# Attention's products on unsplit fp32, P times v in two 64-column halves of the array

## The chip, the cores and the metric

The kernel runs on one core of a Trainium2 chip. Its time is the device time of one execution in microseconds. Three runs of the kernel before took 493.42, 491.84 and 490.93 us; their median is 491.84 us.

## The reference: attention, then two feed-forward blocks

Everything is fp32. Attention has 2 batches of 12 heads, 448 positions and 64 values a head:

```
scores = 0.125 * q @ k.T ; scores above the diagonal = -1e9
attn   = softmax(scores) ; x = attn @ v          -> x: 896 tokens x 768
y      = (sigmoid(x @ w_gate) * (x @ w_val)) @ w_out          (d_ff 1536)
h      = y @ w_in ; s = h * softmax(h)                        (d_ff 1024)
result = (s - mean) / sqrt(var + 1e-6) * g_ln @ w_out2        (896 x 768)
```

## The kernel before, in words

**Split products.** A product of two fp32 operands is made of three matmuls on the type fp32r: each operand is split into a high part and the remainder, and high x high, high x low and low x high are added in PSUM (`TERMS`; the product of the two remainders is left out). So every operand needs a conversion for its high part and a subtraction for its remainder.

**Attention in pairs of heads.** Two heads make a pair; there are 12 pairs. One head lies on partitions 0 to 63, the other on 64 to 127 with its keys in reversed blocks, so that the two score tiles of a pair have causal widths of 64, 192, 320 and 448 columns (`QE`). For each pair the kernel does these steps:

- `load_qk` and `load_v` bring in q, k and v on SP's queue. `prep_k_hi`, `prep_q_hi`, `prep_k_lo`, `prep_q_lo` (lines 234 to 255) split q and k into `qks` on GpSimd, the remainder of q on VectorE. `prep_v_hi` and `prep_v_lo` split v into `v2` (with a zero block of 64 columns between the two heads' columns) and `v3` on GpSimd. For pair 0, and for some steps of pair 1, other engines do it.
- `sc_mm` writes the scores in two groups (widths 448 and 64, then 320 and 192): `sc_mask` (line 354) starts each tile with bf16 matmuls that write the mask, `sc_dots` (line 367) adds three matmuls a tile and head. The two heads use different row halves of the array.
- `sc_max` (line 382; 387 for the first pairs) takes the maxima on VectorE, `sc_exp` (line 394) the exponentials and their sums on ScalarE.
- `sums`, `recips`, `rs_rows`, `rs_bcast` turn the sums into reciprocals and lay them out along the columns by way of a buffer in memory.
- `tr_mm` (line 437) transposes P in four units of four 128x128 blocks; `tr_hi` (line 444) copies a unit's high part to SBUF on ScalarE, `tr_lo` (helper `sub`, line 231) subtracts the remainder on VectorE.
- `pv_mm` (line 468) multiplies by v in eight chunks of in all 21 matmuls over the whole 128 columns of the array: three of 448 columns, and for each of three key blocks and each head three of 384, 256 or 128 columns. For one head's block, the other head's 64 columns of weights are zeros.
- `x_mul` (line 474) multiplies by the reciprocals; `x_hi` (line 223) and `x_lo` split the result into `xy`.

**Order of work.** The order is written out by hand: `STEPS` gives for each engine the step at which a function of pair p is issued, with eight steps a pair (`PER`), and a loop goes through all steps. The first two or three pairs' start is written out ahead of the loop. On TensorE, a period of eight steps holds the scores of pair p, the transposes of pair p - 1 between P times v of pair p - 2. PSUM's eight banks are shared as two for transposes (`ps_t`), two for x (`ps_x`) and two pairs for scores (`ps_s`).

**Weights beside attention.** The feed-forward weights arrive as raw 32-bit words in chunks (768 KB each). `bits_steps` puts the words together on ScalarE and VectorE and asks for the next chunk; `chunk_hi` and `chunk_lo` split it. The first two chunks are asked for at steps 44 and 52; the work on the first four starts at step 88. `early_tiles` (line 500) puts 36 products of the first gate and value tile, those of batch 0, between the last pairs' products, at most two a step. When they are through, the gate and value products proper (line 641) follow.

**After attention** come the gate and value products (line 641), `w_out` (line 671), `w_in` (line 703), the softmax and normalization, and the last product (line 764). All of this is TensorE's without gaps.

Of the kernel before, what the change touches and what calls it, by code (L numbers as in the profile page):

```python
# [23 lines left out]
NQ = 4  # L24
# [19 lines left out]
def attn_moe_moe2(ctx: ExitStack, tc: tile.TileContext, qk, v, w_gv, w_out, w_in2, w_out2, g_ln, out):  # L44
# [48 lines left out]
    pos = {"dma": 0, "bits": 0}  # L93
# [100 lines left out]
    with ExitStack() as actx:  # L194
        qkr = actx.enter_context(tc.tile_pool(name="qkr", bufs=2, side="right"))
        qks = actx.enter_context(tc.tile_pool(name="qks", bufs=2, side="right"))
# [4 lines left out]
        ps_t = actx.enter_context(tc.tile_pool(name="ps_t", bufs=2, space=PSUM, reuse_waits="tile"))  # L201
        ps_x = actx.enter_context(tc.tile_pool(name="ps_x", bufs=2, space=PSUM, reuse_waits="tile"))
# [3 lines left out]
        qk_raw, qk_sp = {}, {}  # L206


        def load_qk(p):
            if p < NH // 2:  # L210
                r = qkr.tile([128, 2, S], F32, tag="qkr", name="qkr")
                both = qk[2 * p:2 * p + 2].rearrange("a d i s -> (a d) i s")
                for i in (1, 0) if p == 0 else (slice(0, 2),):
                    nc.sync.dma_start(out=r[:, i], in_=both[:, i])
                qk_raw[p] = r

        def load_v(p):
            if p < NH // 2:
                nc.sync.dma_start(out=v_raw[p % 2], in_=v[p])

        def on(eng, out, in_):
            if eng == 'A':
                nc.scalar.copy(out=out, in_=in_)
            elif eng == 'P':
                nc.gpsimd.tensor_scalar(out=out, in0=in_, scalar1=1.0, scalar2=1.0, op0=ALU.mult, op1=ALU.mult)
            else:
                nc.vector.tensor_copy(out=out, in_=in_)


        def sub(eng, out, a, b):  # L230
            (nc.gpsimd if eng == 'P' else nc.vector).tensor_tensor(out=out, in0=a, in1=b, op=ALU.subtract)  # L231


        def prep_q_hi(p, eng='P'):
            if eng == 'P':
                nc.gpsimd.tensor_scalar(out=qk_sp[p][:, 1], in0=qk_raw[p][:, 0], scalar1=0.125, scalar2=1.0,
                                        op0=ALU.mult, op1=ALU.mult)
            else:
                nc.scalar.activation(out=qk_sp[p][:, 1], in_=qk_raw[p][:, 0], func=AF.Copy, scale=0.125)

        def prep_k_hi(p, eng='P'):
            qk_sp[p] = qks.tile([128, 4, S], FR, tag="qks", name="qks")
            on(eng, qk_sp[p][:, 0], qk_raw[p][:, 1])

        def prep_k_lo(p):
            sub('P' if p else 'D', qk_sp[p][:, 3], qk_raw[p][:, 1], f32(qk_sp[p][:, 0]))
            if 0 < p < 3:
                load_qk(p + 2)

        def prep_q_lo(p):  # L250
            t = qk_sp[p]
            nc.vector.scalar_tensor_tensor(out=t[:, 2], in0=qk_raw[p][:, 0], scalar=0.125, in1=f32(t[:, 1]),
                                           op0=ALU.mult, op1=ALU.subtract)
            if p > 2:
                load_qk(p + 2)

        def v_parts(p):
            return (v_raw[p % 2][:, 0:3].rearrange("p j (a d) -> p j a d", a=2),
                    *(v2[p % 2][:, i].rearrange("p j (a d) -> p j a d", a=3)[:, :, 0:3:2] for i in range(2)))

        def prep_v_hi(p):
            r, hi, lo = v_parts(p)
            on('P', hi, r)
            on('P', v3[p % 2][:, 0], v_raw[p % 2][:, 3])

        def prep_v_lo(p):
            r, hi, lo = v_parts(p)
            sub('P', lo, r, f32(hi))
            sub('P', v3[p % 2][:, 1], v_raw[p % 2][:, 3], f32(v3[p % 2][:, 0]))
            load_v(p + 2)  # L270
# [3 lines left out]
        v_raw = [one.tile([128, NQ, 2 * D], F32, name=f"vr{i}") for i in range(2)]  # L274
        nc.vector.memset(idle, 0.0)
        warm = one.tile([1, 8], F32, name="warm")
        nc.vector.memset(warm, 0.0)
        nc.scalar.activation(out=warm, in_=warm, func=AF.Exp)
# [19 lines left out]
        zero = one.tile([128, 3 * D], F32, name="zero")  # L298
        nc.vector.memset(zero, 0.0)

        v2 = [one.tile([128, 2, 3, 3 * D], FR, name=f"v2_{i}") for i in range(2)]

        v3 = [one.tile([128, 2, 2 * D], FR, name=f"v3_{i}") for i in range(2)]
# [9 lines left out]
        def zeros(i):  # L313
            for a in range(2):
                nc.scalar.copy(out=v2[i][:, a, :, D:2 * D], in_=zero.rearrange("p (j d) -> p j d", j=3))

# [7 lines left out]
        zeros(0)  # L324
        prep_k_hi(0, 'D')
        prep_q_hi(0, 'A')
        prep_k_lo(0)
        prep_q_lo(0)
# [3 lines left out]
        zeros(1)  # L332
# [4 lines left out]
        def sc_mask(p, g):  # L337
            if p < 2 and g == 0:
                both = [ps_x.tile([128, 512], F32, tag="x", name="s") if p else
                        ps_t.tile([128, 512], F32, tag="t", name="s") for _ in range(2)]  # L340
# [17 lines left out]
        def sc_dots(p, g):  # L358
            t = qk_sp[p]
            flat = t.rearrange("p c s -> p (c s)")  # L360
# [73 lines left out]
        def tr_mm(p, u):  # L434
            ps = ps_tr[p, u] = ps_t.tile([128, 512], F32, tag="t", name="t")
            for c, k in tr_blocks(u):
# [3 lines left out]
        def tr_hi(p, u):  # L440
            if p not in pt_t:
                pt_t[p] = ptp.tile([128, 2, 4, 512], FR, tag="pt", name="pt")
            w = tr_width(u)
            nc.scalar.copy(out=pt_t[p][:, 0, u, :w], in_=ps_tr[p, u][:, :w])  # L444

        def tr_lo(p, u):
            w = tr_width(u)
            sub('D', pt_t[p][:, 1, u, :w], ps_tr.pop((p, u))[:, :w], f32(pt_t[p][:, 0, u, :w]))
# [3 lines left out]
        CHUNKS = ('00 00', '00 11', '11 11', '13 13 13', '21 21', '21 12', '12 12 23', '23 23 22 22 22')  # L452
        pv_terms = {}

        def pv_mm(pr, chunk):
            if chunk == 0:
                ps_pv[pr] = ps_x.tile([128, 512], F32, tag="x", name="x")[:, :S]
                pv_terms.update({w: iter(TERMS) for w in ('00', '11', '12', '13', '21', '22', '23')})
            ps = ps_pv[pr]
            words = CHUNKS[chunk].split()  # L460
            for n, w in enumerate(words):
                sec, j = int(w[0]) - 1, int(w[1])
                a, c = next(pv_terms[w])
                q0 = 128 * j - D if j else 0
                u, c0 = {0: (0, 0), 1: (1 + sec, 0), 2: (3, 256 * sec), 3: (1 + sec, 384)}[j]

                l = v2[pr % 2][:, a, j - 1, (1 - sec) * D:(3 - sec) * D] if j else v3[pr % 2][:, a]
                nc.tensor.matmul(out=ps[:, q0:], lhsT=l, rhs=pt_t[pr][:, c, u, c0:c0 + S - q0],  # L468
                                 start=(chunk == 0 and n == 0), stop=(chunk == 7 and n == len(words) - 1),
                                 skip_group_check=True)  # L470
# [5 lines left out]
        def x_hi(pr):  # L476
            b, m = divmod(pr, NP)
            on('A', xy[m][:, 0, b * S:(b + 1) * S], xf_t[pr])

        def x_lo(pr):  # L480
            b, m = divmod(pr, NP)
            sl = slice(b * S, (b + 1) * S)
            sub('P', xy[m][:, 1, sl], xf_t.pop(pr), f32(xy[m][:, 0, sl]))
# [4 lines left out]
        def early_tiles():  # L488
# [20 lines left out]
        PER = 8  # L509
        early = early_tiles()  # L510
# [5 lines left out]
            *((13 + n, 'E', lambda p, n=n: pv_mm(p, n)) for n in range(len(CHUNKS))),  # L516
            (16, 'A', lambda p: tr_hi(p, 3)), (24, 'A', x_hi, 0, NPR - 1), (22, 'A', x_hi, NPR - 1),
            (1, 'A', lambda p: sc_exp(p, (3,), (0,)), 2),
            (9, 'A', lambda p: tr_hi(p, 0), 1),
            (1, 'A', lambda p: sc_exp(p, (3,), (1,)), 2), (2, 'A', lambda p: sc_exp(p, (0,)), 2),  # L520
            (12, 'A', lambda p: tr_hi(p, 1), 1), (5, 'A', lambda p: sc_exp(p, (2,)), 1),
            (14, 'A', lambda p: tr_hi(p, 2)), (6, 'A', lambda p: sc_exp(p, (1,)), 1),
            (-1, 'D', lambda p: sc_max(p, 3, 0), 2, 3),
            (0, 'D', lambda p: sc_max(p, 3, 0), 3), (16, 'D', lambda p: tr_lo(p, 3)),
# [310 lines left out]
```

## Time and profile before

| | us |
|---|---|
| median of three runs | 491.84 |
| the profiled execution, device time | 492.44 |
| its span | 490.7 |
| busy: TensorE matmul / weight load | 481.4 / 439.8 |
| busy: VectorE / ScalarE / GpSimd | 327.5 / 221.2 / 119.9 |
| moved by DMA | 55.6 MB, 113 GB/s in the mean |

The profile is one execution. The span runs from its first instruction to its last; 1.74 us of the device time lie outside it. Matmuls overlap in the array, so a matmul's own duration is longer than the time until the next one starts, and the busy share of TensorE counts as busy also where it could be denser. The pace of its instructions is read from the chain of waits, which lists for each stretch how long a run of instructions took until the next run began.

### The profile page before, as it was taken

How to read it: one execution, taken by the hardware profiler on the slowest of the kernel's cores; microseconds unless marked ns; L12 is line 12 of the kernel's file. 1: busy time of each engine (PE TensorE's matmuls, PEld its weight loads, DVE VectorE, ACT ScalarE, POOL GpSimd, SP SyncE). 2: the span in 40 equal slices, each digit the busy share in tenths (PEclk: the TensorE clock that was granted, in tenths of full speed). 3: DMA queues.
4: the chain of work that ended last, by engine and by line, in shares of the span. 5: the costliest groups of instructions: out<-in, count | busy, mean ns of one | idle time of the engine just before them, and what ended most of it. 6: DMA issues, size and time to landing. Idle time of an engine off the chain costs nothing.

```text
span 490.7 us, 7583 instructions
## 1 busy us (share of the span) xinstructions
PE 481.4 (98%) x2907; PEld 439.8 (90%) x2907; DVE 327.5 (67%) x508; ACT 221.2 (45%) x471; POOL 119.9 (24%) x190
## 2 busy tenths in 40 slices
PE   8999989899999999999999999999999999999997
PEld 7899878799999999999999999999988888899996
DVE  7888879985757777977777756767725988811110
ACT  6988868753343453453354232343321424333111
POOL 5869597410000000000000000000051778510000
PEclk9999999999999999999999999999999999999999
DMA  6344642233232354453345234453331121001001
GB/s 192 104 158 140 226 132 86 84 126 112 105 128 92 123 172 142 159 170 113 108 168 161 97 107 164 137 160 128 122 127 63 66 86 45 0 33 64 33 32 66
DMA packets 15685, 55.60 MB, mean 113 GB/s; under 512 B 2720, under 2 KB 4768, under 8 KB 15648
## 3 DMA queue, kind: packets, MB, share of 16 engines
q1 hardware_dynamic: 15648, 55.11, 33.9%
q8 instruction: 23, 0.38, 0.3%
q14 instruction: 14, 0.11, 0.1%
HBM read 52.30 MB, written 2.80 MB: 112 GB/s over the span
## 4 chain that ended last, share of the span: by engine, by line
PE 90%; DVE 4%; ACT 3%; DMA 2%; issue 0%; SPq 0%; POOL 0%; ACTq 0%
PE gv L641 34%; PE pm L671 18%; PE po L764 12%; PE h L703 12%; PE x L468 5%; PE t L437 3%; PE s L367 3%; DVE sum L382 2%; PE gv L500 2%; ACT p L394 2%; PE tp L746 1%; DVE pt L231 1%; DMA qkr<-in_qk_dram 1%; PE s L354 0%; DMA rb<-rd 0%
## 5 line engine op out<-in xcount | busy, mean ns | idle before, releaser
L641 PE MATMUL gv<-xy,hl 128*128 128x448 f32 x828 | 168.1, 365 | 0.0
L641 PEld LDWEIGHTS gv<-xy,hl 128*128 128x128 f32 x828 | 155.5, 188 | 12.2
L671 PE MATMUL pm<-g,hl 128*128 128x448 f32 x432 | 87.7, 365 | 0.0
L671 PEld LDWEIGHTS pm<-g,hl 128*128 128x128 f32 x432 | 81.2, 188 | 6.4
L688 POOL TENSOR_SCALAR t<-t,g_sb 128x768 f32<-128x768 f32 x8 | 9.0, 1125 | 247.7 <-PE pm L671 247.7
L134 DVE TENSOR_TENSOR hl<-t,hl 128x768 fp32r<-128x768 f32 x36 | 34.8, 968 | 40.8 <-ACT hl L131 39.0
L764 PE MATMUL po<-wo,lt 128*128 128x384 f32 x336 | 60.7, 340 | 0.0
L703 PE MATMUL h<-wi,xy 128*128 128x512 f32 x252 | 59.3, 396 | 0.0
L764 PEld LDWEIGHTS po<-wo,lt 128*128 128x128 f32 x336 | 58.7, 188 | 0.2 <-POOL wo L693 0.2
L703 PEld LDWEIGHTS h<-wi,xy 128*128 128x128 f32 x252 | 47.1, 188 | 11.4
L117 DVE SCALAR_TENSOR_TENSOR t<-raw,t 128x768 int32<-128x768 int32 (+1 forms) x56 | 52.6, 939 | 1.8
L120 DVE SCALAR_TENSOR_TENSOR t<-raw,t 128x768 int32<-128x768 int32 (+1 forms) x56 | 52.0, 929 | 1.7
L112 ACT ACTIVATE raw<-raw 128x768 f32<-128x768 f32 (+1 forms) x56 | 48.0, 865 | 9.8 <-DMA raw<-in_wo_dram 5.8
L468 PE MATMUL x<-pt,v 128*128 128x384 f32 (+3 forms) x252 | 51.0, 324 | 0.0
L394 ACT ACTIVATE p<-s,sum 128x320 f32<-128x320 f32 (+3 forms) x92 | 43.5, 491 | 11.9 <-DVE sum L382 11.0
L468 PEld LDWEIGHTS x<-pt,v 128*128 128x128 f32 x252 | 37.0, 190 | 1.6
L231 DVE TENSOR_TENSOR pt<-t,pt 128x512 fp32r<-128x512 f32 (+1 forms) x48 | 31.9, 665 | 3.1 <-ACT pt L444 3.0
L171 DVE TENSOR_TENSOR lt<-tp,lt 128x512 fp32r<-128x512 f32 x14 | 9.7, 689 | 36.4 <-ACT lt L170 36.4
L131 ACT CAST hl<-t 128x768 fp32r<-128x768 f32 x36 | 30.0, 833 | 4.8 <-PE pm L671 4.2
L115 DVE TENSOR_SCALAR t<-raw 128x768 int32<-128x768 int32 (+1 forms) x56 | 30.2, 539 | 2.6 <-ACT raw L112 2.6
L183 ACT ACTIVATE wk<-gv 128x448 f32<-128x448 f32 x23 | 11.3, 542 | 44.3 <-PE gv L641 44.3
L382 DVE TENSOR_REDUCE sum<-s 128x2 f32<-128x640 f32 (+3 forms) x44 | 28.3, 683 | 4.0 <-PE s L367 3.9
(97 smaller groups left out, 493.6 us busy)
## 6 DMA issues: line engine op xcount, KB each, us to landing
raw<-in_gv_dram SPq DMA_DIRECT2D x24, 768.0 KB
raw<-in_wo_dram SPq DMA_DIRECT2D x20, 768.0 KB
raw<-in_wi_dram SPq DMA_DIRECT2D x12, 512.0 KB
qkr<-in_qk_dram SPq DMA_DIRECT2D x11, 448.0 KB
vr<-in_v_dram SPq DMA_DIRECT2D x12, 256.0 KB
rb<-rd SPq DMA_DIRECT2D x24, 112.0 KB
out_dram<-o SPq DMA_DIRECT2D x6, 384.0 KB
rd<-rs32q SPq DMA_DIRECT2D x48, 1.0 KB
```

Of the source, the lines that this page charges most:

```text
L112: nc.scalar.activation(out=w1.bitcast(F32), in_=w1.bitcast(F32), func=AF.Copy, scale=2.0 ** -112)
L117: nc.vector.scalar_tensor_tensor(out=tt, in0=w1, scalar=-2 ** 31, in1=tt, op0=ALU.bitwise_and, op1=ALU.bitwise_or)
L120: nc.vector.scalar_tensor_tensor(out=tt, in0=w0, scalar=29, in1=tt, op0=ALU.logical_shift_right, op1=ALU.bitwise_or)
L134: nc.vector.tensor_tensor(out=lo, in0=t_t.pop(it), in1=f32(hi), op=ALU.subtract)
L231: (nc.gpsimd if eng == 'P' else nc.vector).tensor_tensor(out=out, in0=a, in1=b, op=ALU.subtract)
L382: nc.vector.reduce_max(out=sum_t[p % 3][:, 8 + 2 * i:10 + 2 * i], in_=ps_both[p, i], axis=AX.X, negate=True)
L394: nc.scalar.activation(out=p_t[p % 2][:, POFF[i] + (1 - e) * n:POFF[i] + (2 - e) * n], in_=ps_sc[p, i][1 - e], func=AF.Exp, bias=mx, scale ...
L468: nc.tensor.matmul(out=ps[:, q0:], lhsT=l, rhs=pt_t[pr][:, c, u, c0:c0 + S - q0], start=(chunk == 0 and n == 0), stop=(chunk == 7 and n == ...
L641: nc.tensor.matmul(out=ps[i, b], lhsT=w[:, a, cs], rhs=xy[kk][:, x, b * S:(b + 1) * S], start=(kk == 0 and a == 0 and x == 0), stop=(kk == ...
L671: nc.tensor.matmul(out=ps[b], lhsT=w[:, a, cs], rhs=g_t[kk][:, x, b * S:(b + 1) * S], start=(kk == 0 and a == 0 and x == 0), stop=(kk == N ...
L703: nc.tensor.matmul(out=h[:, n * 512:(n + 1) * 512], lhsT=xy[kk][:, a, tk], rhs=wi[n * NK + kk][:, c], start=(kk == 0 and i == 0), stop=(kk ...
L764: nc.tensor.matmul(out=ps[n], lhsT=lts[k // 4][:, a, k % 4], rhs=wo[k][:, c, cs], start=(k == 0 and i == 0), stop=(k == NF2 - 1 and i == 2))
```

## The change

- q and k go into the scores unsplit, as fp32: one matmul for three in `sc_dots`. k is read where it landed; q is scaled by 0.125 into `q_sc`, with 64 columns of zeros ahead of it, which the 128-column weights of the narrowest tile reach into. The conversions and subtractions for q and k are gone.
- v goes into P times v unsplit, from where it landed, and transposed P is copied unsplit: `tr_copy` takes the place of `tr_hi` and `tr_lo`; units 0 and 1 are copied by VectorE, 2 and 3 by ScalarE.
- `pv_mm` has seven matmuls: one of 448 columns over the whole array, and for each of three key blocks one matmul a head with 64 columns of weights, each writing its own half of the partitions.
- Three banks for transposes and one for x, in place of two and two. The first scores of pair 1 take one bank of each.
- Buffers: three of q and k as they land, and three of v, in place of two each.
- Steps move: P times v is issued in two chunks (steps 17 and 18), copies, reciprocals, sums, loads of q, k and v have new steps, and the work on the first weight chunks starts at step 86 in place of 88.
- The first two raw weight chunks are loaded in seven parts at steps 34 to 82, in place of whole at 44 and 52.
- For pair 0, q is loaded ahead of k; VectorE scales it. The 26 small matmuls ahead of the first transposes write into those transposes' own bank.

The diff, cut to its core:

```diff
-    pos = {"dma": 0, "bits": 0}
+    pos = {"dma": 2, "bits": 0}
+    def dma_part(c, lo, hi):
+        if c not in raw_t:
+            raw_t[c] = ring.tile([128, 2 * CH], I32, tag="raw", name="raw")
+        cs = slice(lo * CH // 2, hi * CH // 2)
+        nc.sync.dma_start(out=raw_t[c][:, cs], in_=src[c][0].bitcast(I32)[:, cs])
...
-        ps_t = actx.enter_context(tc.tile_pool(name="ps_t", bufs=2, space=PSUM, reuse_waits="tile"))
-        ps_x = actx.enter_context(tc.tile_pool(name="ps_x", bufs=2, space=PSUM, reuse_waits="tile"))
+        ps_t = actx.enter_context(tc.tile_pool(name="ps_t", bufs=3, space=PSUM, reuse_waits="tile"))
+        ps_x = actx.enter_context(tc.tile_pool(name="ps_x", bufs=1, space=PSUM, reuse_waits="tile"))
...
-                for i in (1, 0) if p == 0 else (slice(0, 2),):
+                for i in (0, 1) if p == 0 else (slice(0, 2),):
...
+        def prep_q(p, eng=nc.gpsimd):
+            eng.tensor_scalar(out=q_sc[p % 2][:, D:], in0=qk_raw[p][:, 0], scalar1=0.125, scalar2=1.0,
+                              op0=ALU.mult, op1=ALU.mult)
...
-                for m, (cq, ck) in enumerate(((1, 0), (1, 3), (2, 0))):
-
-                    for e in range(2):
-                        rows = slice(e * D, (e + 1) * D)
-                        nc.tensor.matmul(out=ps_sc[p, i][1 - e], lhsT=flat[rows, cq * S + n - 128:cq * S + n],
-                                         rhs=t[rows, ck, S - n:] if e else t[rows, ck, :n], start=False, stop=(m == 2), skip_group_check=True)
+                for e in range(2):
+                    rows = slice(e * D, (e + 1) * D)
+                    nc.tensor.matmul(out=ps_sc[p, i][1 - e], lhsT=q_sc[p % 2][rows, n - D:n + D],
+                                     rhs=k[rows, S - n:] if e else k[rows, :n], start=False, stop=True, skip_group_check=True)
...
-        def pv_mm(pr, chunk):
-            if chunk == 0:
+        def pv_mm(pr, *blocks):
+            if 0 in blocks:
                 ps_pv[pr] = ps_x.tile([128, 512], F32, tag="x", name="x")[:, :S]
...
+            for j in blocks:
                 q0 = 128 * j - D if j else 0
...
+                for e in range(2) if j else (0,):
+                    d = slice(e * D, (e + 1) * D) if j else slice(0, 2 * D)
+                    u, c0 = {0: (0, 0), 1: (2 - e, 0), 2: (3, 256 * (1 - e)), 3: (2 - e, 384)}[j]
+                    nc.tensor.matmul(out=ps_pv[pr][d, q0:], lhsT=v_raw[pr % 3][:, (j - 1) % NQ, d],
+                                     rhs=pt_t[pr][:, u, c0:c0 + S - q0],
+                                     start=(j == 0), stop=(j == 2), skip_group_check=True)
...
+        FIRST_RAW = {34: (0, 0, 1), 42: (0, 1, 2), 50: (0, 2, 3), 58: (0, 3, 4),
+                     66: (1, 0, 1), 74: (1, 1, 3), 82: (1, 3, 4)}
...
+            (17, 'E', lambda p: pv_mm(p, 0, 1)), (18, 'E', lambda p: pv_mm(p, 3, 2)),
+            (16, 'A', lambda p: tr_copy(p, 3, 'A')),
+            (1, 'A', lambda p: sc_exp(p, (3,)), 2), (2, 'A', lambda p: sc_exp(p, (0,)), 2),
+            (5, 'A', lambda p: sc_exp(p, (2,)), 1), (6, 'A', lambda p: sc_exp(p, (1,)), 1),
+            (23, 'A', x_hi), (15, 'A', lambda p: tr_copy(p, 2, 'A')),
+            (8, 'D', recips), (-1, 'D', lambda p: sc_max(p, 3, 0), 2, 3), (0, 'D', lambda p: sc_max(p, 3, 0), 3),
             (2, 'D', lambda p: sc_max(p, 2), 2), (3, 'D', lambda p: sc_max(p, 1), 2),
+            (12, 'D', lambda p: tr_copy(p, 0, 'D'), 1), (21, 'D', x_mul), (14, 'D', lambda p: tr_copy(p, 1, 'D'), 1),
+            (7, 'P', sums, 1), (-8, 'P', prep_q, 3), (24, 'P', x_lo),
+            (8, 'S', rs_rows), (8, 'S', rs_bcast), (-2, 'S', lambda p: load_qk(p + 2), 1), (11, 'S', lambda p: load_v(p + 2)),
...
-            if s in (44, 52):
-                dma_next()
+            if s in FIRST_RAW:
+                dma_part(*FIRST_RAW[s])
...
-                e = s - 88 - 8 * c
+                e = s - 86 - 8 * c
```

## Rows read from the trace of the kernel before

**Rows 1.** The page: busy time by engine; granted clock in 40 slices.

```profile
PE 481.4 (98%) x2907; PEld 439.8 (90%) x2907; DVE 327.5 (67%) x508; ACT 221.2 (45%) x471; POOL 119.9 (24%) x190
...
PEclk9999999999999999999999999999999999999999
```

**Rows 2.** Windows: stretch, length, busy us (instructions) by engine, clock, DMA share, GB/s.

```profile
30.32:37.59 7.27, 7.27 (x79) 6.52 (x81) 6.36 (x13) 6.21 (x22) 6.53 (x11) 1.00 0.40 134
...
23.09:83.43 60.34, 58.42 (x601) 52.17 (x602) 51.32 (x97) 48.73 (x165) 46.55 (x71) 1.00 0.46 147
83.43:107.31 23.88, 21.99 (x167) 20.17 (x166) 20.87 (x33) 16.50 (x41) 9.53 (x12) 1.00 0.29 97
107.31:490.70 383.39, 379.92 (x1909) 348.98 (x1907) 237.08 (x336) 137.77 (x204) 47.41 (x73) 1.00 0.32 106
```

**Rows 3.** Waits of TensorE, 23.09 to 83.43 us: total us, times, longest.

```profile
PE t L437 <- DVE pt L231: 1.9, 3, 1.2
```

**Rows 4.** Chain of waits, one period: start us, us until the next, what.

```profile
30.32 0.19 PE s L354 x6
30.51 0.94 PE s L367 x12
31.45 0.13 PE s L354 x8
31.59 0.84 PE s L367 x12
32.42 0.48 PE x L468 x3
32.91 0.46 PE t L437 x4
33.36 0.65 PE x L468 x4
34.01 0.44 PE t L437 x4
34.45 0.94 PE x L468 x8
35.38 0.44 PE t L437 x4
35.82 0.79 PE x L468 x4
36.61 0.63 PE t L437 x4
37.23 0.35 PE x L468 x2
```

**Rows 5.** Chain of waits in the drain: three 128-column products, sixteen gate products.

```profile
99.99 0.28 PE x L468 x3
...
104.08 3.23 PE gv L500 x16
```

**Rows 6.** Groups by shape, 30.32 to 37.59 us: count, busy us, mean ns.

```profile
L444 ACT CAST pt<-t 128x512 fp32r<-128x512 f32 x3 | 1.8, 600 | 0.0
...
L231 DVE TENSOR_TENSOR pt<-t,pt 128x512 fp32r<-128x512 f32 x3 | 2.1, 684 | 0.0
L252 DVE SCALAR_TENSOR_TENSOR qks<-qkr,qks 128x448 fp32r<-128x448 f32 x2 | 1.3, 665 | 0.0
```

**Rows 7.** Chain of waits in the start.

```profile
1.63 4.46 DMA qkr<-in_qk_dram
...
6.11 0.59 ACT qks L239
...
7.35 0.68 DVE mx L387 x2
...
8.12 0.61 ACT p L394
```

**Rows 8.** Timeline of the start: pair 0's q; in brackets the idle time and its releaser.

```profile
3.97 0.58 ACT L239 ACTIVATE qks<-qkr 128x448 fp32r<-128x448 f32 x1 [0.23 <-DMA qkr<-in_qk_dram]
```

More of the change, by code (lines that the diff above doesn't have):

```diff
@@ L218, in load_v @@
             if p < NH // 2:
[L219 to L231, printed above, removed]
@@ L234, in prep_q_hi @@
[L234 to L243, printed above, removed]
@@ L245, in prep_k_lo @@
[L245 to L270, printed above, removed]
+                nc.sync.dma_start(out=v_raw[p % 3], in_=v[p])
+        def prep_q(p, eng=nc.gpsimd):
+            eng.tensor_scalar(out=q_sc[p % 2][:, D:], in0=qk_raw[p][:, 0], scalar1=0.125, scalar2=1.0,
+                              op0=ALU.mult, op1=ALU.mult)
@@ L272, in attn_moe_moe2 @@
         for p in range(2):
             load_qk(p)
-        v_raw = [one.tile([128, NQ, 2 * D], F32, name=f"vr{i}") for i in range(2)]
+        q_sc = [one.tile([128, D + S], F32, name=f"qs{i}") for i in range(2)]
+        v_raw = [one.tile([128, NQ, 2 * D], F32, name=f"vr{i}") for i in range(3)]
         nc.vector.memset(idle, 0.0)
@@ L277, in attn_moe_moe2 @@
         nc.vector.memset(warm, 0.0)
+        for i in range(2):
+            nc.vector.memset(q_sc[i][:, :D], 0.0)
         nc.scalar.activation(out=warm, in_=warm, func=AF.Exp)
@@ L297, in attn_moe_moe2 @@
                                            in1=mask0[rows, rows], op0=ALU.mult, op1=ALU.add)
[L298 to L303, printed above, removed]
         sum_t = [one.tile([128, 16], F32, name=f"sum{i}") for i in range(3)]
@@ L323, in attn_moe_moe2 @@
         keep_warm(ps[:, 0], 31)
[L324 to L328, printed above, removed]
+        prep_q(0, nc.vector)
         load_qk(2)
@@ L338, in sc_mask @@
             if p < 2 and g == 0:
-                both = [ps_x.tile([128, 512], F32, tag="x", name="s") if p else
-                        ps_t.tile([128, 512], F32, tag="t", name="s") for _ in range(2)]
+                both = [ps_x.tile([128, 512], F32, tag="x", name="s") if p and e else
+                        ps_t.tile([128, 512], F32, tag="t", name="s") for e in range(2)]
             else:
@@ L438, in tr_mm, with tr_copy @@
                                     ident if c >= 0 else identx)
-        def tr_hi(p, u):
+        def tr_copy(p, u, eng):
             if p not in pt_t:
-                pt_t[p] = ptp.tile([128, 2, 4, 512], FR, tag="pt", name="pt")
+                pt_t[p] = ptp.tile([128, 4, 512], F32, tag="pt", name="pt")
             w = tr_width(u)
[L444 to L448, printed above, removed]
+            dst, src_ = pt_t[p][:, u, :w], ps_tr.pop((p, u))[:, :w]
+            if eng == 'A':
+                nc.scalar.copy(out=dst, in_=src_)
+            else:
+                nc.vector.tensor_copy(out=dst, in_=src_)
@@ L477, in x_hi @@
             b, m = divmod(pr, NP)
-            on('A', xy[m][:, 0, b * S:(b + 1) * S], xf_t[pr])
+            nc.scalar.copy(out=xy[m][:, 0, b * S:(b + 1) * S], in_=xf_t[pr])
         def x_lo(pr):
@@ L482, in x_lo @@
             sl = slice(b * S, (b + 1) * S)
-            sub('P', xy[m][:, 1, sl], xf_t.pop(pr), f32(xy[m][:, 0, sl]))
+            nc.gpsimd.tensor_tensor(out=xy[m][:, 1, sl], in0=xf_t.pop(pr), in1=f32(xy[m][:, 0, sl]), op=ALU.subtract)
             x_done.add(pr)
```

59 lines of the change are left out of this document (9 added, 50 removed).

## The prediction

> **What bounds the kernel now.** I read the page first: TensorE (PE) is busy in 98% of the span and its granted clock is full in all 40 slices [rows 1]. So time is lost or won by what TensorE is given to do and by the few moments when it waits. The windows by stage [rows 2] show where the change can act. The last 383.39 us (from 107.31 us on) are the two feed-forward blocks, whose code stays; TensorE's list of waits has no entry there. Attention has three stages: a start until the scores of pair 3 begin (23.09 us), eight periods until those of pair 11 begin (60.34 us), and a drain with the first gate products between (23.88 us). The list of waits says how little TensorE waits in the eight periods: 1.9 us in three waits, all of transposes for the subtraction that frees their bank [rows 3]. A period without a wait is in the chain of waits [rows 4], 7.27 us from mask to mask, every piece TensorE's. By kind: masks 0.19 + 0.13 = 0.32 us; scores 0.94 + 0.84 = 1.78 (24 matmuls); transposes 0.46 + 0.44 + 0.44 + 0.63 = 1.97, of which 0.2 in the last group is waiting; P times v 0.48 + 0.65 + 0.94 + 0.79 + 0.35 = 3.21 (21 matmuls). In the same window VectorE is busy 6.36 us, ScalarE 6.21, GpSimd 6.53 [rows 2]: all three would be next if TensorE alone got faster.
>
> **Part by part: TensorE.** The price of a column comes from the four 448-column products of 0.79 us [rows 4]: 0.79 / 1792 = 0.44 ns. A whole-array instruction of 128 columns takes 0.44 / 4 = 0.11 us [rows 4], about twice its 128 columns, so below 250 columns something else, as I read it the weight load, sets the pace. The two heads' score products lie side by side: 448 + 64 columns in three terms are 1536 columns, 0.68 us if the heads overlap and 1.35 if not, and 0.94 was measured.
>
> *How many streams an unsplit product takes* no row shows. Lower end: one, as the four-byte transposes pass at the same 0.11 us as split products of 128 columns. Upper end: four, one for each product of two halves; the kernel's three terms are these without the smallest. I take four, the nearest to the row of three terms, which is the only one of nearly full precision.
>
> The Trainium skill prices the same thing: "FP8 and Floating Point Precision", TensorE Precision Notes, gives a true FP32 product four passes through the array. No run here shows it; by it the period below stays as it is.
>
> Scores: 448 + 64 + 320 + 192 = 1024 columns a head, 4 x 1024 x 0.44 = 1.80 us if the heads lie side by side as now. To it comes what streams don't explain: now 0.94 - 0.68 = 0.26 and 0.84 - 0.68 = 0.16 us a group. With eight matmuls for 24, I take 0.15 a group (ends 0 and 0.26): 2.10 us, 0.32 more than now.
>
> P times v: one whole product of 448 columns and three pairs of halves of 384, 128 and 256: 1216 columns, 4 x 1216 x 0.44 = 2.14 us if halves lie side by side. Were they one after the other, 768 columns more: 3.49. No row shows two column halves; the nearest, the two row halves of the scores, overlap. I take the overlap and, for the run's end where one half still streams alone, 0.22 us: 2.36.
>
> Changing the shape of the array: three 128-column products just behind the scores take 0.48 us [rows 4], three elsewhere 0.28 [rows 5], so going from halves to the whole costs 0.20; the way back shows nothing (0.35 us for two products of 384 columns, with 0.34 to expect). Each pair gains one such change each way: 0.22 us taken, ends 0 and 0.4.
>
> The Trainium skill warns of this: "TensorEngine Tiling (Array Packing)", Tiling Modes, Key Properties, says that changing the mode, not only the tile, drains the engine. The trace agrees, with 0.48 against 0.28 us.
>
> Masks stay (0.32). Transposes stay at 16, 1.76 us without the 0.2 of waiting: a third bank lies between a transpose and the copy that frees it. New period: 0.32 + 2.10 + 1.76 + 2.36 + 0.22 = 6.76 us, 0.51 less than 7.27.
>
> **The other engines.** ScalarE loses two of the four copies of transposed P (0.60 us the wider one [rows 6], the other a little less): 6.2 - 1.1 = 5.1 us a period. VectorE loses four subtractions (2.6, three of them 2.1) and the q remainder (the window holds two, 1.3), and gains the two copies, priced by the subtraction's 0.68 us [rows 6], the nearest row (ends 0.4 and 0.8): 6.4 - 3.9 + 1.3 = 3.8 us. GpSimd loses all splitting of k and v and keeps the scaling of q, the sums and one subtraction, 2 us. All lie under 6.76, so I cost these at nothing; were TensorE below about 5.1 us, ScalarE would bound. One bank for x in place of two: the next pair's whole product waits for this pair's multiplication by the reciprocals. That follows some 2 us behind the halves and has most of a period in hand; behind a late one would stand all of TensorE's queue. On SP's queue the reads of v are now issued where P times v has ended, behind the broadcast of reciprocals; raw weights go in seven parts of 192 to 384 KB for two of 768, and each is issued 8 steps after the last. The third buffers cover both (a pair's q and k are asked for two pairs ahead), so I count nothing, at worst one late landing (some 2 us).
>
> **Start.** The first maximum is taken at 7.35 us: VectorE's queue has pair 1's q remainder ahead of it, which waits for ScalarE's 0.59 us and a transfer that lands at 6.1; the first exponential follows at 8.12 [rows 7]. In the changed kernel nothing of pair 1 stands ahead on either engine. Pair 0's second half is there at 3.97 us [rows 8]; q comes first now, and its scaling (some 0.6) ends about when k lands. Two heads of 512 columns in four streams take 0.9 us and some skew, so the first maximum is at 5.3 and the first exponential at 6.0: 2.1 us earlier. From there ScalarE leads; two copies fewer on it give another 1.1. P times v of pair 0 saves little against longer scores of three pairs. I take -3.0 us (ends -1 and -4.5).
>
> **Drain.** Three P times v save 3 x (3.21 - 2.36 - 0.22) = 1.9, one set of scores adds 0.3. The gate products stay: 0.20 us each (sixteen in 3.23 us [rows 5]), 36 in all. The conversion of the first four weight chunks starts two steps earlier on a VectorE without P's subtractions, but it is also squeezed by a shorter stage (20.87 of 23.88 us busy now [rows 2]); I leave the stage's other waits where they are: -1.6 us (ends -4 and +1).
>
> **Sum.** Start -3.0. Periods: 8 x 6.76 = 54.1, and 1 us of waits kept of 60.34 - 58.16 = 2.2 now: 55.1 - 60.34 = -5.2. Drain -1.6. Together -9.8 us, from the profiled execution's 492.44 (span 490.7 and 1.74 around it): 482.6. The median of the runs is 0.6 lower than the profiled one, so I predict 482.
>
> **Rivals.**
> *Halves of P times v go one after the other* (slower side). The period grows by 1.35 less the 0.2 of skew to 7.9: periods 63.7 (+3.4), start -1.9, drain +1.9, together +3.4: 495 us against the median. It decides once the halves cost 0.5 us more than side by side, for that is all that a period saves. For it: no row shows two column halves at once, and each half needs its own stream of P. Against it: row halves overlap in the scores.
> *An unsplit product takes two streams.* Scores 1.1 us, P times v 1.25, period 4.7 on TensorE; ScalarE's 5.1 and its waits then make 5.4: 8 x 5.4 is 17 less, start -4, drain -4.5: 466. For it: four-byte transposes at 0.11 us. Against it: a transpose needs no arithmetic.
> *TensorE's saving turns into waits*, for copies, late reciprocals through memory, or the first weight chunks: the period falls only to 7.0 with 1 us of waits kept (57 us, -3.3), start -1, drain 0: 488. For it: ScalarE and VectorE have waited for each other in most of these stages, and the drain's VectorE is 87% busy. Against it: both lose work in every period.
> *The scores' heads cease to overlap*, or the longer weight loads of unsplit products stand open: 1.8 us more a pair, period 8.6, 8 x 1.3 less the waits = +9, start and drain +2: 503. For it: below 250 columns the load already sets the pace. Against it: streams grow longer, which covers more load.
>
> **How the numbers follow.** Chances: forecast 0.45, halves in turn 0.17, two streams 0.10, waits 0.18, open loads or heads in turn 0.10. The forecast's own range is 476 to 488. With the unknown streams and halves the range is 469 to 496, which leaves out the 503 and most of the 466. A measurement of this kernel tells 0.5% (2.5 us) from no change. Faster: 0.43 of the forecast, 0.10 of two streams, 0.14 of the waits: 0.67. Same: 0.02 + 0.03 + 0.04 of the halves: 0.09. Slower: 0.13 of the halves, 0.10, 0.01: 0.24.
>
> **What would show it.** In the changed profile's chain: scores of a period near 2.1 us (1.1: two streams; 3.9: heads in turn), P times v near 2.4 (3.5: halves in turn), mask to mask 6.8 us; the halves' two records of one block starting within one stream of each other; the first exponential near 6.0 us; pair 3's scores near 20; the first product of line-641 kind (gate tiles) near 97.5 us, and from there on 383 us as before. The prediction is wrong if an unsplit product is not four streams, if halves don't overlap, or if TensorE's list of waits grows beyond some 4 us in attention.

## The result, and the profile after

The changed kernel took 487.31 us in the median of 12 runs (486.16 to 490.83), the kernel before 492.55 in runs beside it: a ratio of 0.9897 (95% interval 0.9877 to 0.9917). It is 5.2 us faster, about half of the 10 that were forecast. The profiled execution took 489.1 us, 1.8 more than the median, so its stages show somewhat less of the gain.

The windows by stage (stretch, length, busy us and instructions by engine in the order PE, PEld, DVE, ACT, POOL, then clock, DMA share, GB/s); the second and third begin at the masks of pair 3 and of pair 11, and the third ends where the last of the drain's own gate products does, at two closing matmuls of line 181 ahead of the gate tiles' regular loop:

```profile
28.19:34.69 6.50, 6.50 (x64) 4.18 (x66) 4.93 (x10) 5.35 (x21) 1.91 (x3) 1.00 0.45 160
21.68:75.75 54.07, 52.34 (x485) 33.67 (x486) 35.31 (x71) 41.68 (x152) 15.35 (x24) 1.00 0.45 147
75.75:104.06 28.31, 24.12 (x144) 15.60 (x143) 20.53 (x30) 15.27 (x39) 5.42 (x7) 0.88 0.39 132
...
104.06:487.30 383.24, 379.92 (x1908) 348.88 (x1907) 236.16 (x334) 137.65 (x204) 47.41 (x73) 1.00 0.32 106
```

Against [rows 2]: the start is 1.41 us shorter (21.68 for 23.09), the eight periods 6.27 (54.07 for 60.34), the rest equal to 0.15 us; but the drain is 4.43 us longer (28.31 for 23.88), at a mean granted clock of 0.88. Together that is -3.4 us, what the profiled executions differ by (489.1 and 492.44), and the drain is where the rest of the forecast gain went. A period of its own takes 6.50 us, less than the 6.76 that I had worked out.

TensorE's waits in the periods, then in the drain (total, times, longest):

```profile
PE t L381 <- DVE pt L392: 1.7, 3, 1.2
...
PE gv L436 <- ACT hl L137: 2.7, 1, 2.7
PE t L381 <- DVE pt L392: 1.5, 2, 0.7
```

The three waits of the periods stand at 56.6 us (0.16), 64.5 (1.23) and 71.4 (0.33); earlier there is none. So something grows late from period to period. VectorE's waits from 21 to 84 us, so in the periods and the first 8 us of the drain, say what:

```profile
DVE xf L410 <- DMA rb<-rd: 17.1, 7, 3.4
```

It waits for reciprocals, which travel by way of memory: rows of sums are written (L350), then read back by a broadcast (L356), both from SP's queue. SP's timeline (start us, us, engine, line, instruction; L99 a raw weight part, L223 v, L218 q and k), and the chain of waits at the end of the second round:

```profile
66.67 1.09 SPq L356 DMA_DIRECT2D rb<-rd  x2
67.80 0.59 SPq L99 DMA_DIRECT2D raw<-in_gv_dram  x1
68.49 0.38 SPq L223 DMA_DIRECT2D vr<-in_v_dram  x1
68.91 0.42 SPq L218 DMA_DIRECT2D qkr<-in_qk_dram  x1
69.38 1.34 SPq L350 DMA_DIRECT2D rd<-rs32q  x4
73.99 1.09 SPq L356 DMA_DIRECT2D rb<-rd  x2
```

```profile
70.42 3.49 DMA rd<-rs32q
```

The reader is to see a ring: broadcast, three loads (192 + 256 + 448 KB, 0.9 MB), four row writes, and then a hole of 3.3 us, in which SP stands until the rows have landed (3.49 us after the last one's issue began). Only then can the next broadcast go. From broadcast to broadcast that is 73.99 - 66.67 = 7.3 us; the four rounds before it, from the broadcasts at 36.79, 44.02, 51.66, 59.49 and 66.67 us, took 7.2 to 7.8, the two before those, without a raw part, 6.4 and 6.6. TensorE's period is 6.50. So each round with a raw part adds to the lag of the reciprocals, six of the seven waits above and 14.2 of their 17.1 us lying in the eight periods. VectorE waits for them in its queue ahead of P's copies and of the weight words, and from 56 us on TensorE waits too. Over the run SP waits this long for rows (total, times, longest):

```profile
SPq L356 <- DMA rd<-rs32q: 33.2, 15, 3.4
```

The chain in the drain:

```profile
77.27 3.04 DMA rd<-rs32q
...
80.88 3.38 DMA rb<-rd
...
84.38 0.62 DVE xf L410
85.01 0.87 DVE t L126
...
85.90 0.84 ACT hl L137
...
86.79 1.11 PE gv L436 x2
...
88.76 2.97 PE x L404 x6
```

The first weight chunk's last step on VectorE (L126) stands behind a multiplication that waits for reciprocals. TensorE idles for 2.7 us up to 86.79, and then runs at 1.2 GHz: the granted clock is 0.50 from 88 to 92 us, and the first part of P times v takes 2.97 us where its like at 97.68 takes 1.55.

### The profile page after: what moved, and what is told of

It reads as the page before. It is cut to its first block, busy times and chain, and to the rows that moved or that the text cites. A ratio compares the mean times of both kernels' runs of the same rounds, so it can differ in the third digit from the quotient of the medians.

```text
span 487.3 us, 7096 instructions
## 1 busy us (share of the span) xinstructions
PE 476.5 (98%) x2727; PEld 412.7 (85%) x2727; DVE 305.1 (63%) x472; ACT 207.6 (43%) x441; POOL 72.0 (15%) x121
## 4 chain that ended last, share of the span: by engine, by line
PE 87%; DMA 5%; SPq 3%; DVE 2%; ACT 1%; issue 1%; POOL 0%; DVEq 0%; ACTq 0%; POOLq 0%
PE gv L564 34%; PE pm L594 18%; PE po L687 12%; PE h L626 12%; DMA rd<-rs32q 3%; PE x L404 2%; PE gv L436 2%; PE s L309 2%; PE t L381 2%; DMA rb<-rd 1%; PE tp L669 1%; ACT p L336 1%; SPq L350 1%; DVE sum L324 1%; SPq L356 1%
## 5 line engine op out<-in xcount | busy, mean ns | idle before, releaser
L126 DVE SCALAR_TENSOR_TENSOR t<-raw,t 128x768 int32<-128x768 int32 (+1 forms) x56 | 51.2, 913 | 1.6
L336 ACT ACTIVATE p<-s,sum 128x320 f32<-128x320 f32 (+3 forms) x92 | 42.2, 484 | 10.1 <-DVE sum L324 8.1
L121 DVE TENSOR_SCALAR t<-raw 128x768 int32<-128x768 int32 (+1 forms) x56 | 31.2, 557 | 2.8 <-ACT raw L118 2.8
L404 PE MATMUL x<-pt,vr 128*64 128x384 f32 (+3 forms) x168 | 30.5, 425 | 0.0
L309 PE MATMUL s<-qkr,qs 64*128 64x448 f32 (+3 forms) x192 | 28.0, 416 | 0.0
L381 PE MATMUL t<-ident,p 128*128 128x128 f32 x180 | 25.3, 279 | 1.3 <-DVE pt L392 0.9
```

The costliest lines, as they stand in the source:

```text
L126: nc.vector.scalar_tensor_tensor(out=tt, in0=w0, scalar=29, in1=tt, op0=ALU.logical_shift_right, op1=ALU.bitwise_or)
L309: nc.tensor.matmul(out=ps_sc[p, i][1 - e], lhsT=q_sc[p % 2][rows, n - D:n + D], rhs=k[rows, S - n:] if e else k[rows, :n], start=False, st ...
L336: nc.scalar.activation(out=p_t[p % 2][:, POFF[i] + (1 - e) * n:POFF[i] + (2 - e) * n], in_=ps_sc[p, i][1 - e], func=AF.Exp, bias=mx, scale ...
L381: nc.tensor.transpose(ps[:, max(c, 0):max(c, 0) + 128], p_t[p % 2][:, k:k + 128], ident if c >= 0 else identx)
L404: nc.tensor.matmul(out=ps_pv[pr][d, q0:], lhsT=v_raw[pr % 3][:, (j - 1) % NQ, d], rhs=pt_t[pr][:, u, c0:c0 + S - q0], start=(j == 0), stop ...
```

## The experiments

Theory A: SP's round binds. Rivals: B, the weight conversion that starts two steps earlier fills VectorE; C, the loads' bytes delay the small transfers wherever they are issued.

**Loads between rows and broadcast.** `raw_part` issues the weight part that falls to a pair, one a pair from pair 3 on; it, v, q and k go behind the rows' writes, so that these land while SP issues loads. (v goes out five steps later for that, q and k two.)

```diff
-            (8, 'S', rs_rows), (8, 'S', rs_bcast), (-2, 'S', lambda p: load_qk(p + 2), 1), (11, 'S', lambda p: load_v(p + 2)),
+            (8, 'S', rs_rows), (8, 'S', raw_part), (16, 'S', lambda p: load_v(p + 2)), (0, 'S', lambda p: load_qk(p + 2), 1),
+            (8, 'S', rs_bcast),
```

> Edit to the changed kernel: on SP's queue the loads of a period (raw weight part, v, q and k) are issued between the rows of reciprocals and their broadcast, instead of behind the broadcast and so just ahead of the next rows. Theory A (SP's round is the bound: four row writes, 3.2 us until they land behind some 0.9 MB of loads, broadcast, loads; 7.2 to 7.8 us with a raw part against TensorE's 6.50; the late reciprocals hold VectorE, then TensorE, then let its clock fall): rows land within 2 us of the last issue, all eight periods take 6.5 us (52 to 53 in all, for 54.07), the 2.73 us wait for the first weight chunk and the stretch at half clock go, the drain falls from 28.3 to 24 to 25.5 us; 481 to 483 us against 487.3. Theory B (VectorE's weight conversion, started two steps earlier, is what the drain waits for): periods as in A, drain still 27 to 28, 485 to 486. Theory C (the loads' bytes delay the small transfers wherever they are issued): no change, 487.

Measured 480.74 us (0.9747, 0.9709 to 0.9785). Its windows and TensorE's waits:

```profile
21.07:73.11 52.04, 52.04 (x486) 33.51 (x487) 37.94 (x73) 42.26 (x157) 15.34 (x24) 1.00 0.60 184
73.11:95.80 22.69, 21.28 (x143) 14.36 (x143) 19.42 (x28) 14.02 (x33) 5.72 (x7) 1.00 0.38 111
```

```profile
PE gv L436 <- ACT hl L137: 1.4, 1, 1.4
```

And SP's wait for rows, over the run, to set beside the 33.2 us of the changed kernel:

```profile
SPq L356 <- DMA rd<-rs32q: 4.1, 7, 1.6
```

Eight periods of 6.50 us without a wait, the drain 22.7 us at full clock, less than the 24 to 25.5 expected. One of its rounds on SP:

```profile
41.40 1.31 SPq L350 DMA_DIRECT2D rd<-rs32q  x4
42.76 0.36 SPq L99 DMA_DIRECT2D raw<-in_gv_dram  x1
...
44.64 1.09 SPq L356 DMA_DIRECT2D rb<-rd  x2
```

The broadcast goes 1.9 us after the last row is issued (1.5 to 2.2 in the seven rounds with a raw part), and the hole is 0.6 us here. The same instructions on every engine, in another order on one queue, are worth 6.6 us by the medians. B can't explain that, as the conversion starts at the same step. Of C the form falls in which any load costs its time: the same bytes are moved. The changed kernel was not run again beside this one, but two edits below that leave the loads behind the broadcast measured 487.02 and 486.77 us in the same series.

**Raw parts out of the periods.** Both chunks go whole, at the loop's first two steps.

```diff
-        FIRST_RAW = {34: (0, 0, 1), 42: (0, 1, 2), 50: (0, 2, 3), 58: (0, 3, 4),
-                     66: (1, 0, 1), 74: (1, 1, 3), 82: (1, 3, 4)}
+        FIRST_RAW = {0: (0, 0, 4), 1: (1, 0, 4)}
```

> Edit to the changed kernel: the first two raw weight chunks are loaded whole at the first two steps of the loop (about 9 us), so that no raw part is in the eight periods; SP's order is otherwise as in the changed kernel. Theory A: SP's round goes back to the 6.4 to 6.6 us that it took in the changed kernel before the raw parts began, no drift, no wait above 0.3 us for copies; start up to 1 us longer; drain 24 to 25.5; 481 to 484 us. Theory B: drain still 27 to 28, 485 to 486. Theory C agrees with A here (fewer bytes in the periods), so this run speaks on B alone.

481.96 us (0.9769, 0.9730 to 0.9808), as A expects. Without the raw part the rounds from 42 to 69 us take 6.3 to 6.9 us, TensorE waits in none of the periods, and they are 6.50 us again. C agrees with A here, so this run speaks against B alone.

**Raw chunks whole, as before**, at their steps of before.

```diff
+        FIRST_RAW = {44: (0, 0, 4), 52: (1, 0, 4)}
```

> Edit to the changed kernel: the first two raw chunks are loaded whole at steps 44 and 52, as in the kernel before, instead of in seven parts. Theory A: two of SP's rounds take 8.5 to 10 us instead of seven that take 7.2 to 7.8, the lag is about the same (some 5 us) and the other rounds at 6.4 to 6.6 hardly recover it: 486 to 488 us, with the waits for copies starting earlier, about two periods behind step 44. If parts were the whole cause (number of issues, not bytes and order): 483 to 484. Theory B: 487.

487.02 us (0.9881, 0.9834 to 0.9928). Parts or whole makes no difference that these runs can tell. Two rounds of 8.6 and 8.9 us (broadcasts at 42.21, 50.83 and 59.73) build up the same lag as five of 7.2 to 7.8: in both kernels some 4.5 us more than as many periods (17.5 for 13.0, and 37.2 for 32.5). TensorE's waits did not start earlier, as had been expected: the first, of 1.5 us, ends at 64.5 us. This run also shows what the bytes do. From the end of the last row's issue to the broadcast it is 2.8 and 3.0 us in the changed kernel's two rounds with v, q and k alone ahead of the rows, 3.1 to 3.6 in the five after them with 192 KB of raw weights more, 4.5 and 3.9 here with 768 KB, and at most 1.5 to 2.2 with the loads behind the rows. So the rows land later the more was issued just ahead of them. The rest of a longer round is the issue of the raw part itself, 0.69 us (67.80 to 68.49 above).

**Conversion from step 88**, as before.

```diff
+            e = s - 88 - 8 * c
```

> Edit to the changed kernel: the conversion of the first weight chunks starts at step 88, as in the kernel before, instead of 86. Theory A: VectorE is held by late reciprocals either way, so the first gate product waits at least as long: 487 to 489 us. Theory B (the conversion started too early stands ahead of attention's copies): the drain falls by 2 us or more, 484 to 485.

486.77 us (0.9868, 0.9821 to 0.9915), not to be told from the changed kernel. B had forecast 484 to 485. TensorE waits there for a copy on ScalarE (2.5 us) in place of the weight chunk.

**Only the raw parts ahead of the broadcast**; v, q and k stay behind it.

```diff
-            (8, 'S', rs_rows), (8, 'S', rs_bcast), ...
+            (8, 'S', rs_rows), (8, 'S', raw_part), (8, 'S', rs_bcast), ...
```

> Edit to the changed kernel (487.3 us): only the raw weight parts move ahead of the broadcast of reciprocals; v, q and k stay behind it, just ahead of the next rows. Theory A1 (the rows land late because they queue behind bytes issued just ahead of them): the rows have 0.7 MB ahead of them instead of 0.9 to 1.1, and SP's round goes to the 6.4 to 6.7 us of the rounds without a raw part: 481 to 483.5 us. Theory A2 (any load behind the broadcast is too much): rounds of 7 us remain, 485 to 487.

482.07 us (0.9765, 0.9733 to 0.9797): rounds of 6.4 to 7.1 us (broadcasts at 36.53, 42.91, 49.31, 56.39 and 63.09 us), a little longer than the period in the middle; the slack between the engines takes that up, as it does in the kernel with the raw parts early.

**The rows from GpSimd's queue.**

```diff
-                nc.sync.dma_start(out=rows[:, b:b + 32], in_=rs_q[p % 2][b:b + 8])
+                nc.gpsimd.dma_start(out=rows[:, b:b + 32], in_=rs_q[p % 2][b:b + 8])
```

> Edit to the changed kernel: the four row writes are issued from GpSimd's queue instead of SP's; loads and broadcast stay on SP in the same order. Theory A1 with queueing in one queue: rows no longer stand behind SP's loads, land 1.5 to 2.5 us after their issue, SP's round falls by 2 us or more and no longer binds: 481 to 483 us. If it is the shared engines' bytes and not the queue: rows land as late as before (3.2 us), only SP's 1.3 us of issuing goes, round 6.0 to 6.5, 482 to 485. If issuing from GpSimd is dear (some 1 us each): its queue then holds q's scaling and the sums, 485 to 490.

482.03 us (0.9760, 0.9733 to 0.9786). From its timeline (start us, us, engine, line, instruction):

```profile
42.05 2.14 POOL L350 DMA_DIRECT2D rd<-rs32q  x4 [0.78 <-DVE rs32q L345]
...
47.42 1.09 SPq L356 DMA_DIRECT2D rb<-rd  x2
```

The last row is issued at 44.19 and the broadcast goes at 47.42, 3.2 us later. Over the seven rounds with a raw part this is 2.6 to 4.4 us, and it is 3.5 and 3.8 in the two rounds ahead of them, which have none. So rows land late from another queue too, but this run doesn't tell whether the bytes under way hold them, as C has it, or a slower write from GpSimd's queue. What it does show is that the rows no longer wait for their turn behind SP's broadcast and loads: GpSimd issues each set as soon as VectorE has the reciprocals (the bracket), 6.4 to 6.5 us apart. The seven rounds from broadcast to broadcast (35.65 to 81.09 us) take 4.7 to 7.8 us, 6.5 in the mean, TensorE's period.

**Filling the gap.** In the changed kernel, 48 idle matmuls stand ahead of the first accumulation of the first gate tile, in the place where TensorE waits.

```diff
+                keep_warm(both[:, 1], 48)
```

> Edit to the changed kernel (487.3 us): 48 small matmuls on idle data (2.7 us at full clock) stand ahead of each of the first tile's two accumulations, where TensorE waits for the first weight chunk. Their output is overwritten. If the fall of the granted clock to half behind the 2.73 us wait costs what the drain's rows show (P times v's first part 2.97 us for 1.55, in all 2.5 to 3 us): the clock stays full, the second 48 cost up to 2.7 us of their own where TensorE does not wait; net -1 to +0.5, 486 to 488, and the rows of the drain's P times v go back to 1.55 us. If the clock's fall costs nothing by itself (the stretch waits for data anyway): 489 to 490.

485.71 us (0.9830, 0.9779 to 0.9881). The window from 88 to 92 us, and the first part of P times v behind the gap:

```profile
88.00:92.00 4.00, 4.00 (x25) 2.42 (x25) 3.95 (x6) 0.58 (x2) 1.13 (x1) 1.00 0.63 207
```

```profile
87.49 1.55 PE x L404 x6
```

The clock stays at 2.4 GHz and the 2.97 us are 1.55 again, with the wait for data still there. The drain, again up to the two closing matmuls, is 26.0 us for 28.3. So the fall of the clock is a cost of its own, some 2 us in the trace. The expectation said that idle matmuls would stand ahead of a second accumulation too; the edit has one such place only, so nothing is paid back. The net gain is 1.6 us by the medians, which were taken in different series and lie closer than the 2.5 us that the prediction set for telling two times apart.

**Column halves in turn**, on the kernel with the loads between: P times v runs over the heads outside and the key blocks inside, and is issued in one step, not in two.

```diff
-            for j in blocks:
-                q0 = 128 * j - D if j else 0
-                for e in range(2) if j else (0,):
+            for e in range(2):
+                for j in blocks if e == 0 else blocks[1:]:
+                    q0 = 128 * j - D if j else 0
...
-            (17, 'E', lambda p: pv_mm(p, 0, 1)), (18, 'E', lambda p: pv_mm(p, 3, 2)),
+            (17, 'E', lambda p: pv_mm(p, 0, 1, 3, 2)),
```

> Edit to the kernel with the loads between rows and broadcast (480.7 us): P times v issues all three key blocks of one head and then those of the other, so that no two column halves stand next to each other. Theory of the prediction (halves overlap in the array, four streams each): P times v grows from 2.20 to some 3.5 us (768 columns x 4 x 0.44 = 1.35 less 0.1 of skew), the period from 6.50 to 7.75 us; eight periods +10, start +1.2, drain +3.5: 494 to 496 us. Rival (the halves run one after the other already and an unsplit product takes fewer than four streams): no change, 480 to 482.

488.68 us (0.9893, 0.9842 to 0.9944). That is 7.9 us over the kernel with the loads between, less than expected: P times v takes 2.90 us instead of 2.20, 0.70 of the 1.35 that I had worked out, and the period 7.20. So halves do overlap when they alternate, and partly when they don't. The groups of a stretch of 0.08 us show it:

```profile
L404 PE MATMUL x<-pt,vr 128*64 128x384 f32 x1 | 0.5, 537 | 0.0
L404 PE MATMUL x<-pt,vr 128*64 128x256 f32 x1 | 0.4, 379 | 0.0
L404 PE MATMUL x<-pt,vr 128*64 128x128 f32 x1 | 0.3, 273 | 0.0
```

The 384 columns are the second head's first product, the 256 and 128 the last two of the first head, all of which was issued earlier; all three are under way between 48.52 and 48.60 us. The ends of matmuls are modelled in the profile, but the starts say the same: the 384 columns start at 48.24 us, the 256 of the first head at 48.45.

**Banks, both ways.** First two banks for transposes' units and two for x in the kernel with the loads between, then three and one in the kernel before; the first scores of pair 1 take their banks to match.

```diff
-        ps_t = actx.enter_context(tc.tile_pool(name="ps_t", bufs=3, space=PSUM, reuse_waits="tile"))
-        ps_x = actx.enter_context(tc.tile_pool(name="ps_x", bufs=1, space=PSUM, reuse_waits="tile"))
+        ps_t = actx.enter_context(tc.tile_pool(name="ps_t", bufs=2, space=PSUM, reuse_waits="tile"))
+        ps_x = actx.enter_context(tc.tile_pool(name="ps_x", bufs=2, space=PSUM, reuse_waits="tile"))
```

> Edit to the kernel with the loads between rows and broadcast: two banks for transposes and two for x, as in the kernel before, instead of three and one. If the third bank is what keeps transposes from waiting for their copies: 0.2 to 0.6 us of waiting a period, period 6.7 to 7.1, 482.5 to 486 us. If two banks are enough now that copies come sooner: 480.7.

> Edit to the kernel before (492 us): three banks for transposes and one for x instead of two and two, nothing else of the change. If the third bank alone brings what the run with two and two banks lost (8 us): 485 to 490. My theory: one bank for x pays only with P times v in one block; in the kernel before its last products end just ahead of the next pair's first, so TensorE waits in each pair for the multiplication by the reciprocals (0.6 us and its place in VectorE's queue): period 7.27 plus 0.8 to 1.5, 500 to 506 us.

488.92 us (0.9899, 0.9846 to 0.9953) and 504.22 us (1.0213, 1.0189 to 1.0237). With two banks for units the chain of each period goes through VectorE:

```profile
41.92 0.02 issue
41.94 0.62 DVE xf L410
42.56 0.66 DVE pt L392
43.22 0.04 issue
43.27 0.66 PE t L381 x4
```

The fourth transposes wait for a copy that stands behind the multiplication: the period is 7.07 us and the whole 8.2 us over the kernel with the loads between, more than I had allowed. So without the third bank 0.57 of the 0.77 us that a period of 6.50 gains on 7.27 is lost. In the kernel before, three and one cost about 10 us (504.22 against 494.04 beside it; a period of 8.67), the size that I expected. Of its cause only part is seen: TensorE's waits before P times v name GpSimd's split of v (6.8 us), exponentials and a copy (5.9), and the multiplication with 0.7 alone. So the cost is shown, and that the multiplication is behind it is not.

**Two tries at the last 1.41 us**, on the kernel with the loads between: conversion from step 84, and the first gate products from step 97 on.

```diff
-                if s >= PER * NPR and left and next(early):
+                if s > PER * NPR and left and next(early):
```

> Edit to the kernel with the loads between rows and broadcast: the conversion of the first weight chunks starts at step 84 instead of 86. If the 1.41 us that the first gate product still waits there is the conversion's place in VectorE's and ScalarE's queues: the wait falls by 1 us or goes, 479.5 to 480.3 us. If VectorE is full there, the wait moves to transposes (their copies come later): 480.7 or 0.5 longer.

> Edit to the kernel with the loads between rows and broadcast (480.7 us): the first gate products are issued from step 97 on, behind the first transposes of the last pair and the first part of P times v of pair 10, instead of ahead of them at step 96. The 1.41 us that TensorE waits there for the first weight chunk is then covered by 2 us of other work: 479.0 to 480.0 us. If those transposes wait for their copies or exponentials themselves: 480.7.

482.12 us (0.9766, 0.9704 to 0.9828) and 481.42 us (0.9751, 0.9730 to 0.9773): no gain in either. The wait moves to transposes, whose copies VectorE then does later (1.2 us in the second run). VectorE, busy for 19.42 of the 22.69 us of that drain (above), leaves little room; that it is the limit was not tested.

The kernel with the loads between rows and broadcast has the lowest median of all, 480.74 us. Five others, the two tries and the kernels with early raw parts, raw parts ahead and rows from GpSimd, lie within 1.4 us of it, and these runs can't order them; all six beat the changed kernel and the kernel before.

## Why the prediction was wrong, point by point

**Four streams: right.** Each unsplit product stands in the trace as two loads and two matmuls. Scores take 1.00 + 0.94 us (2.10 expected), P times v 2.20 (2.36):

```profile
21.88 1.00 PE s L309 x8
22.88 0.12 PE s L299 x8
22.99 0.94 PE s L309 x8
23.94 0.59 PE t L381 x4
24.53 2.20 PE x L404 x14
26.73 1.46 PE t L381 x12
```

From its streams alone P times v was to take 2.14 us, with halves in turn, so 1984 columns, 3.49. So it is four streams, and halves side by side. The Trainium skill, "FP8 and Floating Point Precision", TensorE Precision Notes, has four passes for true FP32; the trace agrees. The four transposes behind the scores take 0.59 us for 0.44 and the twelve behind P times v 1.46 for 1.32: going from halves of the array to the whole costs some 0.15 us each time. The way back shows in no row by itself. (For the added change, both ways together, 0.22 was taken.) The Trainium skill, "TensorEngine Tiling (Array Packing)", Tiling Modes, Key Properties, says that a change of mode drains the engine; the trace agrees, and gives the size.

**The other engines: under TensorE, as costed.** ScalarE 5.35 us a period (5.1 expected), GpSimd 1.91 (2), VectorE 4.93 (3.8), or 35.31 / 8 = 4.41 in the mean of the eight periods. The sum took too much off: the window before holds a second q remainder by its last 3 ns only, so a period loses one, 0.6 us, and not two: 6.4 - 2.6 - 0.6 + 1.3 = 4.5. It didn't matter in the periods; that it left VectorE less with which to catch up in the drain was not tested.

**Periods: -6.3 us for -5.2.** Right in its mechanism, and close in part because two misses offset each other: a period without waits takes 6.50 us for 6.76, 2.1 us less in eight, and waiting adds 2.1 us (54.07 less 8 x 6.50) for the 1 that was kept.

**Start: -1.4 us for -3.0.** The first exponential came at 7.60 us, not 6.0, as the first eight score matmuls took 2.16 us from 4.55 on. The same code took 1.34 and 1.40 us in two runs of other kernels, whose first exponential came at 6.77 and 6.84; there the start is 21.07 and 20.83 us, 2.0 and 2.3 less than before (the kernels with the loads between and with the raw parts early). It is TensorE's pace that differs, as the first group of scores shows beside one in a period:

```profile
4.55 2.16 PE L309 MATMUL s<-qkr,qs 64*128 64x448 f32 x8
28.22 1.17 PE L309 MATMUL s<-qkr,qs 64*128 64x448 f32 x8
```

The 31 idle matmuls ahead of the first scores take 3.49 us, 0.11 each, in these runs and in the kernel before, where the 48 in the filled gap took 2.84, 0.06 each. So TensorE starts at about half its later pace and keeps it for longer in some executions. In the run with conversion from step 84 the first group takes 1.16 us at once, the first exponential comes at 6.56, and the start is 20.55 us, 2.5 less than before. The column of granted clocks reads 1.00 over all of this; what makes the difference stays open.

**Drain: +4.4 us for -1.6. This is the step that failed**, and with it the sentence that costs SP's queue at nothing ("so I count nothing, at worst one late landing (some 2 us)"). I had looked at whether each buffer would be free and not at how long SP's queue takes for one round. The round was there to be read before: SP waits there for rows 21.5 us in ten waits between 23 and 83 us, and the two rounds with raw chunks, between the broadcasts at 44.23, 53.43 and 62.25 us, take 9.2 and 8.8 us, the next, without one, 6.9. With a period of 7.27 us VectorE waited for reciprocals in none of the eight. The chunks cost something even so: two periods, from 52.07 and 59.95 us, took 7.88 and 9.06 us, and GpSimd waited 2.9 and 3.2 us there for q and k that were issued behind a chunk. The change shortens the period and puts a load of raw weights into seven rounds. The runs that shorten the round take the loss back: with the loads between rows and broadcast the drain is 22.69 us (22.28 expected), the whole 480.7 (482). The prediction's own sign of being wrong came up: TensorE's waits in the periods and the drain are 1.7 + 2.7 + 1.5 = 5.9 us, above the 4 named there, for 3.7 in the kernel before.

**The rivals.** Halves in turn, two streams, and heads in turn or open loads are excluded by 2.20 us for P times v and 1.00 + 0.94 for the scores. The nearest was that TensorE's saving turns into waits for late reciprocals (488 us), but not as it was put there, with a period of 7.0 us: the period keeps its gain and the debt falls due at the end, made larger by the clock. That its 488 lies so near the 487.3 is in part luck.

## What to carry to other kernels

When a change shortens a loop's period, add up each queue's round as well, with its waits inside: a queue that waits for its own small transfers to land is an engine like any other, and it binds as soon as its round exceeds the new period. Put bulk loads behind the small transfer that somebody waits for, not just ahead of it. A lag that grows by a fraction of a microsecond a period is seen only at the end, so compare the last periods with the first ones.

## What the runs showed of the hardware

The broadcast that waits for four small row writes could go 2.8 to 3.0 us after the last was issued behind 0.7 MB of loads, 3.1 to 3.6 behind 0.9 MB, 3.9 to 4.5 behind 1.4 MB, and after 1.5 to 2.2 with the loads behind them; issued from GpSimd's queue, 2.6 to 4.4. A wait of 2.7 us was followed by a granted clock of 0.50, and 48 idle matmuls in its place left it at 1.00. At the start 31 idle matmuls took 0.11 us each, later ones 0.06, with the granted clock at 1.00 over both. Products for the two column halves overlapped even when one head's were all issued ahead of the other's: a later one began ahead of the earlier head's last.
